# Five loads of 14, 9, 5, 3 and 1 row blocks in place of six of 10, 8, 6, 4, 2 and 2 for the last weight of a decode kernel

## The chip, the core and the metric

The kernel runs on one core of one Trainium2 chip. The metric is the time of one execution on the device, in microseconds (us); lower is better. Before the change three runs gave 127.64, 127.74 and 127.87 us, so the median is 127.74 us. A profile of one execution stands beside them. Engines are named as the profile names them: PE (TensorE, matmuls; PEld is its weight load), DVE (VectorE), ACT (ScalarE), POOL (GpSimd) and SP (SyncE, which here only issues loads). "SPq" is SP's instruction queue.

## The reference, cut to what matters

One token `x` of 576 numbers goes through two branches, and both results are added to it. Branch A is attention over the last 4096 positions of a cache with 16 key/value heads and 32 query heads; branch B is a gated feed-forward block. Everything is bf16 in memory.

```python
def _A_ref(x, k_cache, v_cache, wq, wo):
    q = (x @ wq) ...                                  # 32 heads of 128
    k = jnp.repeat(k_cache[:, :, Sk - W:, :], 2, axis=1)   # W = 4096
    v = jnp.repeat(v_cache[:, :, Sk - W:, :], 2, axis=1)
    p = _softmax(einsum('bhqd,bhkd->bhqk', q, k) * Dh ** -0.5)
    o = einsum('bhqk,bhkd->bhqd', p, v)
    return o.reshape(B, Sq, Hq * Dh) @ wo             # (1, 4096) @ (4096, 576)

def _B_ref(x, w_in, w_sp, b_sp, w_out):
    z = _gelu(x @ w_in)
    z1, z2 = z[..., :Fh], _layernorm(z[..., Fh:])     # Fh = 2304
    return (z1 * (w_sp * z2 + b_sp)) @ w_out          # (1, 2304) @ (2304, 576)

xn = _layernorm(x)
return x + _A_ref(xn, ...) + _B_ref(xn, ...)
```

The change concerns how `wo`, 4096 x 576, comes into the core. That matrix is the last thing the answer is multiplied with.

## The kernel before

**What is moved.** The core reads 50.96 MB: `wq`, `w_in`, 8 tiles of keys and 8 of values of 2048 KB each, `w_out` (2592 KB) and `wo` (4608 KB). One DMA moves one tile, every one of these is issued by SP, and all of them go through one queue (q1 in the profile). SP issues them in the order in which lines 98 to 111 write them: `wq`, two key tiles, `w_in`, keys and values in turn, `wout`, and last the pieces of `wo`.

**The ring.** All these tiles share a ring of 7 slots of 18 x 576 numbers per partition (`RING`, `SLOT`, the pool `ring`). A load past the seventh waits until an earlier tile's readers are done, and takes the slot that comes free. SP issues in order, so a load that waits holds back the loads behind it. In the profiled execution `wout` was issued at 81.44 us, when both value tiles of the second group of heads had been used, and the six pieces of `wo` at 85.86, 95.64, 100.32, 100.75, 113.93 and 114.35 us. They took the slots of key tile 6, key tile 7, value tiles 4 and 5, and value tiles 6 and 7, in that order: the first two waited for the transposes at line 268, the next two for the matmuls `pv(2)` at line 344, the last two for `pv(3)`.

**Row blocks of `wo`.** `load_n` (lines 93 to 96) views `wo` as 128 partitions x 32 row blocks x 576 columns. Partition p holds rows 32p to 32p+31; a row block t is row 32p+t of every partition. One row block is 128 x 1152 bytes, 144 KB. A load of n row blocks from `lo` on moves, for each partition, one run of n x 1152 bytes, starting lo x 1152 bytes into that partition's part of the matrix.

**What uses them.** The last stage of the kernel adds up the answer in two accumulators in PSUM, `acc[0]` for columns 0 to 287 and `acc[1]` for the rest. `out_mms` (lines 465 to 468) issues one matmul into each, at different columns of the PE array. For branch B `out_hv` does this for the 18 row blocks of `wout`; then lines 488 and 489 run over the 32 row blocks of `wo` in order, with `Y` (the attention result, its last quarter written by `y_copy(3)`) as the other operand. The first matmul of each piece waits for that piece's DMA. After the last one DVE and ACT copy the two halves of the answer to `res` (lines 492 and 493), SP stores it (line 494), and at line 520 SP waits once more for the counters of all queues and engines before the cores' engines meet at the end.

**Counters.** Each DMA signals a counter (semaphore). The loads of SP use eight counters in rotation; a DMA that uses all 16 DMA engines shows sixteen completions in the trace, one for each engine, and has landed with the last of them. The store of the answer, with one partition, ends with one completion.

Of the kernel before, what the change touches and what calls it, by code (L numbers as in the profile page):

```python
# [39 lines left out]
def kernel(  # L40
# [52 lines left out]
    def load_n(src, per, lo, n, name):  # L93
        v = ring_tile(f"{name}{lo}", n, D)
        nc.sync.dma_start(v, src.rearrange("(p t) n -> p t n", t=per)[:, lo:lo + n, :])
        return [(lo + t, v[:, t, :]) for t in range(n)]
# [10 lines left out]
        V[m] = load_kv(A_v_cache, m, "v")  # L107
    wout_sb = load_n(B_w_out, NF, 0, NF, "wout")
    wo_sb = []
    for n in (10, 8, 6, 4, 2, 2):  # L110
        wo_sb += load_n(A_wo, 32, len(wo_sb), n, "wo")


# [411 lines left out]
```

## Time and profile before

The profiled execution took 127.7 us on the device by its own clock; its span, from the first to the last instruction, is 125.9 us, and some 1.8 us lie around it. The median of the runs is 127.74 us.

| view | what it gives | value |
|---|---|---|
| busy time of the span | PE, DVE, ACT, POOL | 54%, 61%, 27%, 7% |
| DMA queues | q1's packets, as a share of 16 engines' span | 95.3% |
| stretches, 112 to 114 and 118 to 120 us | data moved | 422 and 415 GB/s |
| trace, last completion of `wout` | | 112.03 us |
| trace, last completion of the `wo` pieces of 10, 8, 6, 4, 2, 2 | | 115.28, 118.02, 120.08, 121.46, 122.14, 122.83 us |
| trace, median completion (8th of 16) of the same pieces | | 113.79, 116.50, 118.58, 120.03, 120.74, 121.41 us |
| timeline | first matmul with `wo`, last matmul ends | 116.89, 123.28 us |

How to read it: a row of forty digits has one digit for each fortieth of the span (3.15 us). The chain of waits follows the work that ended last back from the end, from each piece to what released it. A line of the timeline gives start, length, engine, line, operation and tiles, and in brackets how long the engine had been idle and what ended that.

### The profile page before, as it was taken

The numbers are of one execution on the slowest core, as the hardware profiler recorded it, in microseconds if no ns is written. First come the engines' busy times: TensorE is split into PE (matmuls) and PEld (weight loads), VectorE is DVE, ScalarE is ACT, GpSimd is POOL, SyncE is SP. The second block draws the span as 40 slices with busy tenths as digits, with TensorE's granted clock in tenths as the row PEclk, the third lists the DMA queues.
The fourth block names the chain that finished last, engine by engine and source line by source line (L and its number), as shares of the span: only waits on it lengthen the run. The fifth ranks groups of instructions, "written<-read, shape, count | busy, mean of one in ns | idle before, by whom it ended". The sixth has DMA issues, their size and how long they took to land.

```text
span 125.9 us, 1614 instructions
## 1 busy us (share of the span) xinstructions
PE 67.8 (54%) x618; PEld 30.9 (25%) x618; DVE 77.3 (61%) x149; ACT 33.6 (27%) x85; POOL 8.2 (7%) x28
## 2 busy tenths in 40 slices
PE   0002841089999977069356049648039711187861
PEld 0001301021299922014111012411012511024530
DVE  6704135999353896793898298899098967005001
ACT  1200011000036590000441930260950183910001
POOL 3991000000000000100000000000000000000000
PEclk9999999999996557856999959967756995559999
DMA  4999999999999999999999999999999999999950
GB/s 130 417 427 437 432 422 442 419 426 433 435 429 427 442 416 416 437 437 432 437 422 432 437 427 432 432 416 437 437 424 437 427 426 453 409 416 415 419 226 0
DMA packets 4127, 51.06 MB, mean 406 GB/s; under 512 B 534, under 2 KB 536, under 8 KB 1048
## 3 DMA queue, kind: packets, MB, share of 16 engines
q1 hardware_dynamic: 4034, 50.96, 95.3%
q8 instruction: 5, 0.08, 0.2%
q10 hardware_dynamic: 86, 0.00, 0.0%
q14 instruction: 2, 0.02, 0.0%
HBM read 50.96 MB, written 0.00 MB: 405 GB/s over the span
## 4 chain that ended last, share of the span: by engine, by line
DMA 56%; PE 16%; DVE 14%; ACT 7%; issue 3%; SPq 1%; POOL 0%; ACTq 0%
DMA k<-in_A_k_cache_dram 43%; DMA x<-in_A_x_dram 7%; DMA wo<-in_A_wo_dram 7%; DVE kT L268 6%; PE ops L344 6%; PE S L277 5%; ACT PT L321 4%; PE qps L227 3%; ACT pz L305 2%; DVE Qb L255 2%; DVE pt L315 2%; DVE q_rep L238 1%; ACT q_rep L236 1%; DVE on L358 1%; PE lps L327 1%
## 5 line engine op out<-in xcount | busy, mean ns | idle before, releaser
L277 PE MATMUL S<-kT,Qb 128*8 128x512 bf16 x128 | 32.5, 638 | 29.0 <-DVE kT L268 29.0
L268 DVE STREAM_TRANSPOSE kT<-k 128x1024 f32<-128x1024 f32 x32 | 36.9, 1212 | 6.9 <-DMA k<-in_A_k_cache_dram 6.8
L305 ACT ACTIVATE pz<-S,nm 64x1024 bf16<-64x1024 f32 x8 | 11.3, 1409 | 45.1 <-DVE nm L301 30.4
L321 ACT COPY PT<-pt 32x64 f32<-32x64 f32 x64 | 18.9, 296 | 14.3 <-DVE pt L315 13.6
L277 PEld LDWEIGHTS <-Qb 128*8 128x8 bf16 x128 | 6.4, 96 | 48.4 <-issue 45.4
L344 PE MATMUL ops<-v,PT 128*16 128x512 bf16 x128 | 11.7, 451 | 3.5 <-ACT PT L321 3.5
L315 DVE STREAM_TRANSPOSE pt<-pz 128x1024 bf16<-128x1024 bf16 x8 | 9.4, 1214 | 4.2 <-ACT pz L305 4.2
L380 PEld LDWEIGHTS <-win 128*128 128x128 bf16 x162 | 10.1, 169 | 0.9 <-issue 0.9
L380 PE MATMUL zps<-XT,win 128*128 128x2 bf16 x162 | 10.2, 202 | 0.0
L354 DVE SCALAR_TENSOR_TENSOR om<-ops,rs,dmask 128x512 f32<-128x512 f32 x4 | 3.0, 742 | 7.1 <-PE ops L344 7.1
L298 DVE TENSOR_REDUCE mx<-S 128x1 f32<-128x1024 f32 x4 | 4.9, 1222 | 3.8 <-PE S L277 3.8
L344 PEld LDWEIGHTS <-PT 128*16 128x16 bf16 x128 | 5.0, 98 | 7.4 <-ACT PT L321 4.1
L467 PE MATMUL acc<-wo,Y 128*1 128x288 bf16 x64 | 4.7, 285 | 1.7 <-DMA wo<-in_A_wo_dram 1.6
L194 PE MATMUL ps_x<-x,rmat 64*128 64x9 bf16 x1 | 0.2, 164 | 9.4 <-DMA x<-in_A_x_dram 9.4
L236 ACT CAST q_rep<-qps 128x512 bf16<-128x512 f32 x2 | 1.2, 585 | 14.7 <-DVE q_rep L238 14.7
L227 PE MATMUL qps<-wq,XT 128*2 128x512 bf16 x36 | 4.0, 626 | 1.0 <-DVE XT L218 1.0
L492 DVE CAST res<-acc 1x288 bf16<-1x288 f32 x1 | 0.4, 446 | 6.6 <-PE acc L467 6.6
L358 DVE TENSOR_REDUCE on<-om 128x128 f32<-128x512 f32 x4 | 4.1, 1036 | 0.1
L238 DVE CAST q_rep<-qps 128x512 bf16<-128x512 f32 x2 | 1.4, 692 | 4.6 <-PE qps L227 3.9
L327 PE MATMUL lps<-lx,lsum 128*128 128x1 f32 x8 | 2.2, 343 | 3.2 <-DVE Y L372 3.2
L493 ACT CAST res<-acc 1x288 bf16<-1x288 f32 x1 | 0.4, 389 | 12.7 <-PE acc L467 12.7
L467 PEld LDWEIGHTS <-Y 128*1 128x1 bf16 x64 | 2.8, 83 | 3.4 <-issue 2.5
(90 smaller groups left out, 44.6 us busy)
## 6 DMA issues: line engine op xcount, KB each, us to landing
k<-in_A_k_cache_dram SPq DMA_DIRECT2D x8, 2048.0 KB, 24.3
v<-in_A_v_cache_dram SPq DMA_DIRECT2D x8, 2048.0 KB, 24.8
win<-in_B_w_in_dram SPq DMA_DIRECT2D x3, 1728.0 KB, 23.3
wout<-in_B_w_out_dram SPq DMA_DIRECT2D x1, 2592.0 KB, 30.6
wq<-in_A_wq_dram SPq DMA_DIRECT2D x1, 2560.0 KB, 8.7
wq<-in_A_wq_dram SPq DMA_DIRECT2D x1, 2048.0 KB, 13.0
wo<-in_A_wo_dram SPq DMA_DIRECT2D x1, 1440.0 KB
wo<-in_A_wo_dram SPq DMA_DIRECT2D x1, 1152.0 KB
```

What stands on the lines that cost most here:

```text
L227: nc.tensor.matmul(qps[32 * g:32 * g + 2, :], lhsT=XT[:, s, :], rhs=wv[:, 512 * g:512 * (g + 1)], start=(s == 0), stop=(s == NS - 1), tile ...
L268: nc.vector.transpose(dst[:, 1024 * n:1024 * (n + 1)], src[:, 1024 * n:1024 * (n + 1)])
L277: nc.tensor.matmul(S[g % 2][32 * i:32 * i + 8, hf, :], lhsT=Qb[:, 2 * m + hd, be].rearrange("p a h -> p (a h)"), rhs=kv[:, be // 2, be % 2 ...
L298: nc.vector.tensor_reduce(out=mx[:, 0:1], in_=s[:], op=ALU.max, axis=mybir.AxisListType.XY)
L305: nc.scalar.activation(p[lo:hi, :, :, hd], s[lo:hi].rearrange("p a (t r) -> p (a t) r", r=16), ACT.Exp, bias=nm[lo:hi, 0:1], scale=SCALE, ...
L315: nc.vector.transpose(dst[:, 1024 * n:1024 * (n + 1)], src[:, 1024 * n:1024 * (n + 1)])
L321: nc.scalar.copy(PT4[32 * a:32 * a + 32, i % 2, i // 2, :], pt4[32 * i:32 * i + 32, :, a])
L327: nc.tensor.matmul(lps[:, 0:1], lhsT=lsum[:].rearrange("p q c x h -> p (q c x h)"), rhs=lx[:, g:g + 1], start=True, stop=True)
L344: nc.tensor.matmul(ops[32 * q:32 * q + 16, :], lhsT=d["PT"][:, pr, t0:t0 + 4].rearrange("p t x h -> p (t x h)"), rhs=V[2 * g + pr][:, t0:t ...
L358: nc.vector.reduce_sum(on[:], om[:].rearrange("p c d -> p d c"), axis=AXX)
L380: nc.tensor.matmul(zps[:, :, t], lhsT=wt[:, t, :], rhs=XT[:, s, :], start=(s == 0 and t == 0), stop=(s == NS - 1 and t == NF - 1), skip_gr ...
L467: nc.tensor.matmul(acc[n], lhsT=lhs[:, col:col + 1], rhs=wv[:, CW * n:CW * (n + 1)], start=False, stop=last, tile_position=(0, 32 * n))
```

## The change

One tuple of sizes at line 110 is replaced. The 32 row blocks are loaded in the same order and by the same queue, and the matmuls that use them stay in the same order.

```diff
     wo_sb = []
-    for n in (10, 8, 6, 4, 2, 2):
+    for n in (14, 9, 5, 3, 1):
         wo_sb += load_n(A_wo, 32, len(wo_sb), n, "wo")
```

The pieces begin at row blocks 0, 14, 23, 28 and 31, where they began at 0, 10, 18, 24, 28 and 30.

## The prediction

> **What bounds the kernel now.** I read the page's row of DMA shares first, then the chain of waits at its end, then the timeline of PE in the last 7 us, and last the closing waits of SP.
>
> ```profile
> DMA  4999999999999999999999999999999999999950
> q1 hardware_dynamic: 4034, 50.96, 95.3%
> q8 instruction: 5, 0.08, 0.2%
> ```
>
> The 16 DMA engines are full from the first slice to the 38th. What is loaded, not when it is asked for, sets the end. The chain ends so:
>
> ```profile
> 110.74 3.36 PE ops L344 x23
> ...
> 114.34 8.49 DMA wo<-in_A_wo_dram
> 122.83 0.04 issue
> 122.87 0.45 PE acc L467 x4
> 123.33 0.43 DVE res L492
> ```
>
> The chain walks from the last piece of wo back to its issue at 114.34 and from there to the matmuls of line 344, as if an earlier issue would help. It would not: 8.49 us is far more than 288 KB need. The piece stood in a full queue. The trace's completions show how that queue drains: wout's last completion at 112.03, then the six pieces' at 115.28, 118.02, 120.08, 121.46, 122.14, 122.83. The last five steps are 2.74, 2.06, 1.38, 0.68 and 0.69 us for 8, 6, 4, 2 and 2 row blocks: 0.343 us per row block each time, and no visible price of a piece. The earlier loads of 2048 KB end 4.85 us apart, 0.341 us for 144 KB. So the last byte arrives when the slowest DMA engine has worked off its share of everything.
>
> Now PE behind the landings:
>
> ```profile
> 116.89 2.37 PE L467 MATMUL acc<-wo,Y 128*1 128x288 bf16 x36
> 120.12 0.90 PE L467 MATMUL acc<-wo,Y 128*1 128x288 bf16 x12 [0.87 <-DMA wo<-in_A_wo_dram]
> 121.50 1.10 PE L467 MATMUL acc<-wo,Y 128*1 128x288 bf16 x12 [0.48 <-DMA wo<-in_A_wo_dram]
> 122.87 0.41 PE L467 MATMUL acc<-wo,Y 128*1 128x288 bf16 x4 [0.28 <-DMA wo<-in_A_wo_dram]
> ```
>
> PE needs 0.122 us for a row block (36 matmuls, 18 pairs, 2.37 us less the 0.29 of the last one, over 17 steps), a third of the 0.343 that the row block takes to arrive. It waits at each piece, starts 0.04 to 0.05 us after the landing, and finishes before the next. Only what it does after the last landing lies on the path.
>
> And the end, line 520:
>
> ```profile
> L520 SPq EVENT_SEMAPHORE  x7: 17/28/657, 124.2 to 125.8; - x7
> L520 SPq DRAIN  x3: 7/7/13, 125.2 to 125.5; - x3
> SPq L520 <- DMA out_dram<-res: 0.7, 1, 0.7
> ```
>
> The first five of these instructions check ten counters, two each, in a fixed order. The third (124.336, 0.657 long) contains the counter of the answer's store and waits for it until 124.993. The fourth and fifth, at 125.03 and 125.09, find all done, and the drain follows at 125.156.
>
> **The change part by part.**
>
> *Issue.* The pieces should take the slots in the order in which they came free before: 14 blocks at 85.86, 9 at 95.64, 5 at 100.32, 3 at 100.75, 1 at 113.93. Only one row block now waits for pv(3), instead of four. Worth nothing: at 113.93 the queue holds row blocks that keep it busy for 8 us more, and the fastest engine finished the piece of 4 blocks only at 119.51. The cover is that backlog; if it were gone, the piece issued at 113.93 would be late by its whole wait. One issue of SP (0.33 to 0.38 us) and its wait go away at 114.3, where SP has nothing to do until 123.79: zero. No wait is added, on SP, ACT's or POOL's queue.
>
> *The bytes* are the same, in the same order. One piece fewer saves eight packets' overhead and a completion on each engine. The slowest engine's steps give 0 for a piece; the mean over the sixteen completions gives 3.43, 2.75, 2.06, 1.40, 0.73 and 0.70 us, against 0.341 per row block 0.02 more for each large piece. I take -0.02 us; bounds 0 and -0.08 (a packet of 2304 bytes lasts 0.093 us in the trace but they follow each other every 0.086; eight such differences and a completion of 0.009 if none were hidden).
>
> *Small last packets.* The last piece's packets have 1152 bytes, and no load before has such. The nearest rows are the answer's store, one packet of 1152 bytes, 0.051 us, and the 2304-byte packets, 0.093 us: the difference is the bytes' time. So in proportion, 0; bounds 0 and +0.34 us, if 128 packets of 1152 bytes took as long as 128 of 2304 (0.685 a piece). I take 0, since the row of the right size lies on the line.
> In this trace every load starts at a multiple of 256 bytes (row blocks 0, 10, 18, 24, 28, 30; one is 4.5 x 256). The Trainium skill, "DMA: Bandwidth & Descriptors", section "How a descriptor splits into AXI transactions", speaks against the new cuts: a read that does not begin on a 256-byte boundary also fetches the bytes before it, and pays their beats. Row blocks 23 and 31 begin 128 bytes past one, so by the rule two pieces carry 128 bytes more in each packet, 8 x 128 bytes per engine, by the 2304-byte packets' pace some 0.038 us each, estimated: the sum would be 0.08 smaller, 127.58 us. No run here shows a load so placed.
>
> *Landings.* From 115.28 for ten blocks, at 0.343 a block: 14 blocks at 116.65, the second piece at 119.74, the third 121.46, the fourth 122.49, the last 122.83, less 0.02. PE is ready for wo at 116.89, so the larger first piece still comes 0.2 before it is wanted, and were it later PE has a second to catch up (14 x 0.122 from 116.89 ends at 118.6, the next landing is 119.74).
>
> *PE's tail.* Before: the last piece starts at 122.874, its second pair at 122.995, and the last matmul ends at 123.283. After: the piece of three starts 0.045 after 122.49, at 122.535, takes three pairs of 0.122 and frees PE at 122.90; the last row block has landed by then (122.83 + 0.045 = 122.875), so the last pair starts at 122.90 instead of 122.995. That is -0.095 us; bounds -0.12 (a pair) and 0. DVE, ACT and the store follow unchanged.
>
> *The closing waits.* The loads use eight counters in turn. With one DMA fewer, the store of the answer takes the counter that the last wo piece had before, one place earlier in the turn: not the one in the third check but one that sits in the fifth. If the order of checks stays, the first four are done during the store, and the drain comes 0.037 after the answer has landed (the gap behind an instruction here), at 124.993 + 0.037 = 125.03 instead of 125.156: -0.126 us. Bounds -0.126 and 0.
>
> Sum: -0.02 - 0.095 - 0.126 = -0.24 us. The profiled execution, 125.91 of span and 1.8 around it, 127.70 in all, would be 127.46; the median of the runs lies 0.04 above it, so 127.50, 0.19% faster. What a measurement of this kernel can tell from no change is about 0.2%, 0.26 us, so 127.48 divides "faster" from "same", and the forecast lies on that edge.
>
> **Rivals.** *The checks at the end follow the new order of counters.* For it: the order is chosen when the kernel is built, and the trace shows one instance. Then only -0.115 is left: 127.63 us.
>
> *Small packets cost a fixed time.* The last landing moves by +0.34 to 123.15, PE starts its last pair at 123.20 instead of 122.995, +0.2, less 0.126: 127.82 us, or 127.95 with the rival above as well. Against it: the 0.051 us packet. The Trainium skill's "Perfetto Trace Analysis", section "DMA Optimizations", says that DMAs under 2 KB pay a significant overhead per transfer; the packets' durations here do not bear that out.
>
> *A block of PE's code meets a late engine (slower).* Engines are not equally late. The sixteen completions of a load lay 0.52 us apart until 28 us and 1.45 us from 33 us on; the jump follows a packet of code at 29.63, and each 16 KB packet on q8 (36.33, 44.72, 77.98, 110.01) makes one more engine late. When wo ends, eleven engines are done by 121.65 and five at 122.28 to 122.83. The fifth such packet, at 121.55, delayed none, because its engine had finished. If the piece sizes put that block, or the moment PE asks for it, on one of the five while it still holds wo, a packet of that size on q1 lasts 0.61 us, so +0.6: 127.50 + 0.60 = 128.10 us. It decides from the point where the fetch comes before that engine's last wo packet. Against it: PE's instructions do not move, and with row blocks 23 to 27 released at 121.5 as 24 to 27 were, PE gets to the same place in the code at the same time or up to 0.12 later.
>
> *Nothing comes through* (the checks in new order and the last landing late by as much as PE gains) would be 127.74, and is inside the second and third.
>
> **How the numbers follow.** Chances: forecast 0.68, checks in new order 0.13, small packets 0.07, code 0.12. Around each lies the spread of the runs, 0.23 us over three. The forecast's own range is 127.35 to 127.62, and the low bounds of the packets and of PE's tail lie below the taken values, so I put 0.44 of its 0.68 under 127.48 and 0.24 over. The order of checks gives 0.02 and 0.11. Small packets: 0.05 same and 0.02 slower. Code: 0.12 slower. Together 0.46 faster, 0.40 same, 0.14 slower. The range leaves out the code case and the forecast's thin low end: 127.50 - 0.09 (the two unused bounds, 0.06 and 0.025) - 0.11 (half the spread) = 127.30; up to the small packets' 127.82, 127.85.
>
> **What would show it.** Five landings near 116.65, 119.74, 121.46, 122.49 and 122.81; PE idle before row blocks 14, 23 and 28, and not before 31; the last matmul ending near 123.17; the drain 0.04 after the landing of the answer. A last landing after 123.0 would make the prediction wrong: with equal steps in the sixteen completions it is packets, with one engine alone it is code. A gap in the DMA share before 121 us would say that the backlog argument is false.

## The result and the profile after

The changed kernel takes 127.50 us (median of 14 runs, 127.31 to 127.64) against 127.65 us for the kernel before (14 runs, 127.48 to 127.87) measured beside it: ratio 0.9984, interval 0.9977 to 0.9992. Two further comparisons gave 0.9985 (0.9973 to 0.9998) and 0.9983 (0.9973 to 0.9994). The medians differ by 0.15, 0.22 and 0.20 us, and three comparisons agree on a gain, though each alone is at the edge of what can be told.

The profiled execution took 127.54 us with a span of 125.66, against 127.70 and 125.91. First the page's rows of DMA share and of queues:

```profile
DMA  4999999999999999999999999999999999999960
q1 hardware_dynamic: 3890, 50.96, 95.5%
q8 instruction: 5, 0.08, 0.2%
```

The DMA engines are as full as before, up to the same slice. The packets on q1 fall from 4034 to 3890, by 144: one load fewer is 128 packets of data and 16 completions. Then the end of the chain of waits (start, length, what):

```profile
100.85 21.59 DMA wo<-in_A_wo_dram
122.44 0.04 issue
122.49 0.71 PE acc L467 x8
123.19 0.43 DVE res L492
```

The chain now goes back to the piece of three row blocks, issued at 100.85, not to the last one. The eight matmuls of the last two pieces follow each other without a gap that the chain shows: the last pair starts 0.133 us after the pair before it, where two pairs of one piece are 0.122 apart. The same in PE's timeline:

```profile
116.60 1.88 PE L467 MATMUL acc<-wo,Y 128*1 128x288 bf16 x28
119.67 1.27 PE L467 MATMUL acc<-wo,Y 128*1 128x288 bf16 x18 [1.18 <-DMA wo<-in_A_wo_dram]
121.41 0.78 PE L467 MATMUL acc<-wo,Y 128*1 128x288 bf16 x10 [0.47 <-DMA wo<-in_A_wo_dram]
122.49 0.66 PE L467 MATMUL acc<-wo,Y 128*1 128x288 bf16 x8 [0.30 <-DMA wo<-in_A_wo_dram]
```

PE waits before row blocks 14, 23 and 28, as forecast, and longer than before in sum (1.95 against 1.63 us); that idle time is not on the path. And the closing waits of SP at line 520 (count, then shortest, median and longest in ns):

```profile
L520 SPq EVENT_SEMAPHORE  x7: 17/28/28, 124.1 to 125.6; - x7
L520 SPq DRAIN  x3: 7/7/7, 124.9 to 125.2; - x3
```

with SP's wait for the answer's store in the view of waits (sum, number, longest):

```profile
SPq L520 <- DMA out_dram<-res: 0.6, 1, 0.6
```

None of the checks is 0.657 us long any more: the wait for the answer now lies before the fifth check, which is recorded with its own 28 ns, and the drain follows it.

The trace's own times, in us, side by side:

| | before | forecast | after |
|---|---|---|---|
| last completions of the pieces | 115.28, 118.02, 120.08, 121.46, 122.14, 122.83 | 116.65, 119.74, 121.46, 122.49, 122.81 | 116.54, 119.62, 121.36, 122.44, 122.82 |
| start of the last pair of matmuls | 122.995 | 122.90 | 122.863 |
| completion of the answer's store | 124.97 | | 124.83 |
| drain behind it | 125.156 | 0.04 after the store by the text, 0.06 by its figures | 124.914 |
| from the store's completion to the drain | 0.186 | | 0.081 |

### The profile page after: what moved, and what is told of

Its sections match the earlier page's. It is cut to its first block, busy times and chain, and to the rows that moved or that the text cites. A ratio compares the mean times of both kernels' runs of the same rounds, so it can differ in the third digit from the quotient of the medians.

```text
span 125.7 us, 1612 instructions
## 1 busy us (share of the span) xinstructions
PE 67.3 (54%) x618; PEld 30.8 (25%) x618; DVE 77.3 (62%) x149; ACT 33.6 (27%) x85; POOL 8.2 (7%) x28
## 3 DMA queue, kind: packets, MB, share of 16 engines
q1 hardware_dynamic: 3890, 50.96, 95.5%
## 4 chain that ended last, share of the span: by engine, by line
DMA 67%; PE 14%; DVE 12%; issue 3%; ACT 1%; SPq 1%; POOL 0%
DMA k<-in_A_k_cache_dram 43%; DMA wo<-in_A_wo_dram 17%; DMA x<-in_A_x_dram 7%; DVE kT L268 6%; PE S L277 5%; PE qps L227 3%; PE ops L344 3%; DVE Qb L255 2%; DVE q_rep L238 1%; ACT q_rep L236 1%; DVE on L358 1%; PE lps L327 1%; PE acc L467 1%; DVE om L354 1%; PE ps_x L204 0%
## 5 line engine op out<-in xcount | busy, mean ns | idle before, releaser
L344 PE MATMUL ops<-v,PT 128*16 128x512 bf16 x128 | 11.2, 430 | 3.5 <-ACT PT L321 3.5
```

The source lines that it names most:

```text
L344: nc.tensor.matmul(ops[32 * q:32 * q + 16, :], lhsT=d["PT"][:, pr, t0:t0 + 4].rearrange("p t x h -> p (t x h)"), rhs=V[2 * g + pr][:, t0:t ...
```

## The experiments

The differences are of the size of the spread, so each is read twice: in the times, and in the profile, where a step of 0.1 us is plain. Completions and starts that no view above prints are read from the same traces.

**Six loads with a one-block end, twice.** This has the new end and the old number of loads.

```diff
-    for n in (14, 9, 5, 3, 1):
+    for n in (13, 8, 5, 3, 2, 1):
```

> Six pieces of 13, 8, 5, 3, 2 and 1 row blocks: the number of loads of before, the one-block end of after. My theory (two gains, 0.1 us in PE's tail and 0.126 us in the closing waits): the last landing stays at 122.8, the last pair of matmuls starts 0.045 after it (122.87, against 122.995 before), but the store uses the third check's counter again and two checks follow its landing, so only the tail's gain is left: about -0.12 us against before, 127.53, ratio 0.9991. Rival (the closing waits give nothing, all of the gain is the shorter last piece): as fast as the changed kernel, -0.15 to -0.2 us, and the closing waits of the two look alike. Rival (the gain comes from having one load fewer, be it in the queue or at the end): no gain, 127.65, with a last landing as before or later.

> Pieces of 13, 8, 5, 3, 2, 1 once more: six loads, one-block end. Its first profile showed the tail's gain (last pair at 122.90 against 122.995) and its first times none. My theory (the gain in the tail is real and counts in the runs): ratio 0.999, 0.1 us behind the changed kernel. Rival (only the number of loads counts, the tail is lost in how the last landing scatters): ratio 1.0, as in its first runs, 0.15 us or more behind the changed kernel.

Measured: 127.69 us against 127.67, ratio 1.0000 (0.9991 to 1.0009), and the second time 127.55 against 127.76, ratio 0.9984 (0.9976 to 0.9993). The two do not agree with each other; my -0.12 us lies between them, and the times alone don't decide. Beside the changed kernel itself, measured with the second of them at 127.54, this one is 0.01 us behind, not the 0.1 that I expected. The profiles separate the two terms: last completions at 122.85 and 122.76, last pair 0.043 and 0.042 us later, as in the changed kernel (0.044; before 0.164). The closing check is the long one again, here the checks at line 520 in the first of the two profiles:

```profile
L520 SPq EVENT_SEMAPHORE  x7: 17/28/658, 124.1 to 125.7; - x7
```

From the store's completion to the drain it takes 0.186 and 0.185 us.

**Five loads with a two-block end, twice.** This has the old end and the new number.

```diff
-    for n in (14, 9, 5, 3, 1):
+    for n in (12, 8, 6, 4, 2):
```

> Five pieces of 12, 8, 6, 4 and 2 row blocks: the number of loads of after, the two-block end of before. My theory: the last pair of matmuls starts 0.12 us after the first pair of the last piece as before (122.99), the tail gains nothing; the store's counter sits in the fifth check, the drain comes 0.04 after that check ends, -0.126 us and some 0.02 for the piece: 127.51, ratio 0.9989. Rival (the one-block end is all of it): 127.65, ratio 1.0, with the drain 0.18 us after the answer's landing as before.

> Pieces of 12, 8, 6, 4, 2 once more: five loads, two-block end. Its first profile showed the closing checks in the order of the changed kernel, 0.126 us shorter. My theory: ratio 0.999, as the first time (0.9993). Rival (only the one-block end counts): ratio 1.0, as slow as before.

Measured: ratio 0.9993 (0.9984 to 1.0001), then 0.9988 (0.9979 to 0.9996), near the forecast 0.9989; beside the changed kernel's 127.54 the second is 127.61. In both profiles the last pair starts 0.16 us after the last completion (122.89 and 123.052; 123.16 and 123.32), as before the change, and the drain comes 0.08 us after the store, as after it. The checks at line 520 in the first of the two profiles:

```profile
L520 SPq EVENT_SEMAPHORE  x7: 17/28/28, 124.3 to 125.8; - x7
```

**The first piece in two loads.** Nothing in the program differs from the changed kernel but the number of loads, and through it the counter of the store.

```diff
-        nc.sync.dma_start(v, src.rearrange("(p t) n -> p t n", t=per)[:, lo:lo + n, :])
+        for a, b in ((0, 7), (7, 14)) if n == 14 else ((0, n),):
+            nc.sync.dma_start(v[:, a:b, :], src.rearrange("(p t) n -> p t n", t=per)[:, lo + a:lo + b, :])
```

The base, on the same chip:

> The changed kernel a third time, as the base of the next two. My theory: 0.15 to 0.25 us under before, ratio 0.998 to 0.9988.

> The changed kernel with its first piece of 14 row blocks loaded by two loads of 7 into the same tile, so that there are six loads again and nothing else differs at the end: same last landing, same tail. My theory: the store takes the third check's counter, two checks follow it, and the drain comes 0.126 us later after the answer's landing; the 7-block loads cost 0.02 us: 0.13 to 0.15 us behind the changed kernel, ratio to before about 0.9993. Rival (the checks' place is worth nothing in the times of whole runs): level with the changed kernel.

Measured: the base 127.54 us (0.9983), the split one 127.75 us (0.9999, interval 0.9989 to 1.0009): 0.21 us behind, where 0.13 to 0.15 were forecast. Its profile has the long check back (line 520 is 521 here):

```profile
L521 SPq EVENT_SEMAPHORE  x7: 17/28/655, 124.4 to 126.1; - x7
```

and 0.186 us from store to drain, which by the profiles is worth 0.186 - 0.081 = 0.105 us. I had expected the same end of the queue in both, and it was not the same: the last landing is at 123.16 in this profile and 123.05 in the base's, and the last pair starts 0.092 us after it instead of 0.041, because the last row block came only 0.315 us after the piece of three, less than PE needs for three pairs. So the whole runs are 0.21 us apart and agree with the closing checks, but they don't show that term alone; whether the split or the scatter of single executions moved the landing is open.

**One row block per load.** `load_n` issues one load for each number in `cuts`, all into one tile (its loop is left out of the cut below).

```diff
+        cuts = {14: (5, 5, 4), 5: (1,) * 5, 3: (1,) * 3}.get(n)
+        wo_sb += load_n(A_wo, 32, len(wo_sb), n, "wo", cuts)
```

> The changed kernel with the same five tiles, but the last nine row blocks come by nine loads of one row block each (packets of 1152 bytes, every second one starting 128 bytes past a 256-byte boundary), and the first tile by three loads, so that there are thirteen loads and the store keeps the counter it has after the change. My theory (a packet costs its bytes, a load some 0.01 to 0.02 us): steps of 0.343 to 0.36 us between the last completions of the nine, last landing 122.8 to 123.0, 127.5 to 127.7 us. Rival (reads that start off a 256-byte boundary pay for the bytes before it): the steps of row blocks 23, 25, 27, 29, 31 are about 0.038 us longer than those of 24, 26, 28, 30, +0.2 us in all. Rival (a small packet costs as much as one of 2304 bytes): steps near 0.68 us, the last landing 3 us later, 130.5 us.

Measured: 128.64 us, ratio 1.0072 (1.0058 to 1.0085), so the time missed my forecast. The steps up to row block 29 did not. From 119.78 the last completions lie at 120.15, 120.53, 120.88, 121.26, 121.64, 122.02 and 122.41: row blocks 23, 25, 27 and 29 took 0.37, 0.35, 0.38 and 0.39 us, row blocks 24, 26 and 28 took 0.38 each. A row block alone costs 0.376 us against 0.343 in a large piece, so a load of 1152-byte packets costs 0.03 us more than its bytes. It does not cost 0.685, and odd row blocks are not dearer than even ones. The Trainium skill's rule on reads that start off a 256-byte boundary ("DMA: Bandwidth & Descriptors", section "How a descriptor splits into AXI transactions"), which by estimate would have added 0.038 us to each odd one, does not show here; the trace decides against it at this size of packet. In the changed kernel's own trace all packets of 1152 bytes last 0.051 us, those of row block 31, which starts off such a boundary, too.

Then row blocks 30 and 31 come late. SP's waits (times in us: sum, number, longest) and PE's timeline:

```profile
SPq L97 <- DMA wo<-in_A_wo_dram: 6.4, 4, 2.8
SPq L97 <- DMA wout<-in_B_w_out_dram: 6.0, 1, 6.0
```

```profile
119.82 2.92 PE L472 MATMUL acc<-wo,Y 128*1 128x288 bf16 x32 [0.76 <-DMA wo<-in_A_wo_dram]
123.66 0.64 PE L472 MATMUL acc<-wo,Y 128*1 128x288 bf16 x4 [0.91 <-DMA wo<-in_A_wo_dram]
```

With thirteen loads on eight counters, SP holds each of the later loads until the load that had its counter has landed. Row block 30 was issued at 119.80, right after the nine-block piece had landed on its counter at 119.78. Its first completion came 0.85 us after that of row block 29, where 0.38 is the pace: the early engines had run dry. This is what becomes of the cover when the backlog is gone. Its last completion came 1.20 us after that of row block 29, but that is one engine of the sixteen, 0.84 us behind all others (123.61; the next at 122.77, which is on pace). So most of the time lost, 0.84 of some 1.1 us, is that one engine, and the nine small loads at 0.03 us each make up the rest, as an estimate; the engines that ran dry did not set the landing. A code packet started at 121.36; that it is what held the late engine fits the executions below, but the trace names no engine for a packet.

**More code for PE.** 60 matmuls with a zero column, which add zeros to the answer, in the step `j == 10` of the loop (the lines that set up the column `zz` are left out).

```diff
+        if j == 10:
+            for i in range(60):
+                nc.tensor.matmul(acc[i % 2][:, 0:128], lhsT=zz[:, 0:1], rhs=ident[:],
+                                 start=False, stop=False, tile_position=(0, 32 * (i % 2)))
```

> The changed kernel with 60 further matmuls of a zero column (120 PE instructions) in the tenth step of the loop, where PE has idle time; they add zeros to the answer. Their code moves every later 16 KB packet of code to an earlier time, the fifth one from 110 to 100 or before and the sixth from 121 to 110 or so. My theory (each such packet makes one DMA engine late by 0.5 to 0.7 us, and one not late before, as all so far did): six late engines at the end instead of five, the last landing within 0.1 us of 122.82, 127.4 to 127.7 us. Rival (such a packet can fall on an engine that is late already): five late engines, one of them 0.6 us later, last landing 123.4, 128.1 us. Rival (code packets have nothing to do with late engines): five late engines and the same end.

Measured: 127.57 us, 0.9992 (0.9983 to 1.0002), last landing 122.92. The fourth 16 KB packet came at 91.50 and the fifth at 119.62, where the changed kernel's first profile has them at 110.43 and 120.70 (the expectation counts the 8 KB packet at 29 us too, so they are its fifth and sixth; the last came later than its 110). At the end six engines are more than 1.2 us behind the first, where the changed kernel has five (counting one at 1.02). How far each of the sixteen is behind the first, in us, the six latest, from this kernel's completions:

```text
load landed at  90.88:  0.52 0.62 1.37 1.64 1.68 1.69
load landed at  95.78:  0.74 1.29 1.52 1.57 1.58 1.63   (a code packet at 91.50, another of 8 KB at 93.74)
load landed at 119.48:  0.55 1.31 1.47 1.57 1.59 1.61
load landed at 121.65:  1.28 1.47 1.55 1.58 1.61 2.03   (a code packet at 119.62)
load landed at 122.92:  1.29 1.48 1.59 1.61 1.62 1.87
```

After each of these two 16 KB packets one more engine is late, as the theory said, and the first of these steps moved from 110 to 91.5 with its packet. But what it costs that engine is some 1.5 us (by the rows, an estimate: one near 0.5 has gone, one at 2.03 has come), not the 0.5 to 0.7 of my expectation, and the last one fell behind all others, so a late packet set the landing (122.92; the others were done at 122.67).

**The changed kernel once more**, on the chip of the two repeats above.

> The changed kernel once more, beside the next two on the same chip, since the differences are of the size of the spread. My theory: -0.15 to -0.25 us against before (ratio 0.998 to 0.999), and 0.1 us ahead of each of the next two. Rival (the change is worth nothing and the first comparison was chance): ratio 0.9995 to 1.0005.

Measured: 127.54 us, 0.9985 (0.9973 to 0.9998). Its profiled execution was its slowest, 128.10 us, with a last landing at 123.45 instead of 122.82:

```profile
120.33 1.27 PE L467 MATMUL acc<-wo,Y 128*1 128x288 bf16 x18 [1.23 <-DMA wo<-in_A_wo_dram]
122.12 0.78 PE L467 MATMUL acc<-wo,Y 128*1 128x288 bf16 x10 [0.52 <-DMA wo<-in_A_wo_dram]
123.14 0.65 PE L467 MATMUL acc<-wo,Y 128*1 128x288 bf16 x8 [0.24 <-DMA wo<-in_A_wo_dram]
```

Every landing is 0.6 to 0.7 us later than in the first profile of the same kernel, and the completions, given as above, say from where:

```text
load landed at 105.69:  0.60 0.76 0.94 1.28 1.60 1.61 1.91
load landed at 112.41:  0.59 0.74 1.26 1.63 1.64 1.89 2.48   (a code packet at 109.80)
load landed at 123.45:  0.59 0.72 1.26 1.64 1.65 1.89 2.48
```

The engine at 0.94 is gone and one at 2.48 has come: the packet met an engine that was already behind, so it need not make one more engine late. In the first profile the packet of that time met one of the early engines, and the last engine stayed at 1.78. Which engine it meets differs between executions of one kernel.

**An uneven load.** The three-block piece by partitions 0 to 87 and 88 to 127.

```diff
-        nc.sync.dma_start(v, src.rearrange("(p t) n -> p t n", t=per)[:, lo:lo + n, :])
+        rows = src.rearrange("(p t) n -> p t n", t=per)
+        for p0, p1 in ((0, 88), (88, P)) if lo == 28 else ((0, P),):
+            nc.sync.dma_start(v[p0:p1], rows[p0:p1, lo:lo + n, :])
```

> The changed kernel with the piece of three row blocks loaded by two loads, partitions 0 to 87 and 88 to 127. By the Trainium skill (DMA: Bandwidth & Descriptors, section on why a DMA increments its semaphore by 16) a load of 88 partitions uses the 11 lowest engines and one of 40 the 10 lowest, so engines 11 to 15 would carry nothing of this piece and engines 0 to 9 half as much again, 0.5 us. The look is to show whether the five late engines are among the low ones. If all five are: eleven completions for the first part with five late ones, the last landing 0.5 us later, 128.0 us. If none is: no late one among the eleven, the late engines skip 1.03 us, last landing about 122.3, 127.0 us. Rival (all 16 engines take part in any load): sixteen completions each, nothing moves.

One run: 129.43 us, slower than either forecast. The two parts had eleven and ten completions of data, as the Trainium skill's page says ("DMA: Bandwidth & Descriptors", the section on why a DMA increments its semaphore by 16). But the completions did not keep their order of lateness: already the five-block piece ahead, which was not touched, ended at 122.88 instead of 121.36, with 3.32 us between its first and last engine. So the run doesn't tell whether the late engines are among the low ones, and why the load ahead spread out so much stays open.

**The store issued by ACT.**

```diff
-    nc.sync.dma_start(out.flatten_outer_dims(), res[:])
+    nc.scalar.dma_start(out.flatten_outer_dims(), res[:])
```

> The changed kernel with the store of the answer issued by ACT, which makes one half of it, instead of SP. My theory: ACT's copy ends 0.02 us before DVE's, the issue still waits for DVE, and SP's counter check before it falls away, so the store starts up to 0.05 us earlier; it ends on a counter of ACT's loads, whose place among the checks decides: 0.1 us faster than the changed kernel if it is the last, 0.1 slower if two checks follow. Rival (the issue on ACT takes as long as on SP and the place is the same): level.

Measured: 127.48 us, 0.9981 (0.9970 to 0.9993), beside 127.54 and 0.9983 for the changed kernel: not to be told apart, as the rival said. The store did not start earlier (0.076 us after DVE's copy ends, 0.074 in the changed kernel's first profile), and it sits on the same last counter as when SP issues it, so ACT's issues take their counters from the same rotation; the drain comes 0.08 us after it in both. The kernel beats the one before, and is no proven gain over the change.

## Why the prediction was right, point by point

The forecast was 127.50 us and -0.24 us; the runs gave 127.50 and, over the three comparisons, -0.15, -0.22 and -0.20 us. In the profiled span the change is -0.25 us. That the median is met to the hundredth is luck: the kernel before measured 0.09 us less than the 127.74 from which the forecast started, and the gain beside it was 0.09 less than forecast. The span is met by luck in part: the last landing of the changed kernel is at 122.82, 123.45 and 123.05 in its three profiles, and the first of them happens to match the 122.83 before. By the prediction's own sign, a last landing after 123.0, the other two would have spoken against it; the sign took no account of this scatter. What is not luck is the two steps behind the last landing, which the experiments show one by one.

- **The bound.** The queue is full and drains at one rate, so the last landing does not depend on the pieces. Right for the mean of the sixteen completions of the last piece: 121.69 before; 121.68, 121.79 and 121.78 after; 121.77 and 121.69 with six other pieces, 121.68 and 121.69 with five. The last completion scatters more than any cut moved it: 122.83 before; 122.82, 123.45 and 123.05 after; 122.85 and 122.76 with six pieces, 122.89 and 123.16 with five. In the first profile the forecast of the five landings is off by 0.01 to 0.12 us.
- **Issue and backlog.** Worth nothing while the backlog covers it. Right; the one-row loads show the other case, where a load issued 2.6 us ahead of the end of the backlog left the early engines without work for some 0.5 us (0.85 less 0.38).
- **One piece fewer, small packets.** -0.02 and 0 were taken; -0.01 is the difference of the two landings in the first pair of profiles, far inside their scatter. A piece of one row block costs 0.03 us more than its bytes, which takes back the piece saved. The bound of -0.08 does not follow from its working: eight times 0.007 and 0.009 are 0.065.
- **PE's tail.** -0.095 was taken, with -0.12 as a bound; the start of the last pair against its last landing went from 0.164 to 0.044, which is -0.120. The small last piece is the cause: the step is there with six pieces and a one-block end (0.043, 0.042) and gone with five and a two-block end (0.165, 0.164). The forecast had PE busy until 122.90; the piece of three landed at 122.44, not 122.49, so PE was free in time and only the last landing counted. That is close: with a last row block 0.315 us behind the piece of three, in the kernel with the split first piece, 0.092 was left.
- **The closing waits.** -0.126 was taken, -0.105 is measured. The order of the checks stayed, and the store's counter moved from the third to the fifth. In all thirteen profiles the drain comes 0.185 or 0.186 us after the store's completion where the counter is in the third check, and 0.081 or 0.082 where it is in the fifth. What I left out is the fifth check itself, which still has to run after the wait (0.028 us); and the 124.993 from which I counted is the end of the third check, 0.023 after the landing.
- **The three terms** are 0.01, 0.120 and 0.105 in the first pair of profiles, together 0.24 us; the whole runs gave a little less. The store's own duration differs by less than 0.01 us between the two profiles (from its issue to its completion 1.13 us in each).
- **The rival of the code packets** was mis-sized and partly misplaced. A 16 KB packet costs an engine some 1.5 us (0.94 to 2.48 above), not 0.6, and not only the one at 121 us can hurt: in the execution that landed at 123.45 the one at 110 decided how late the last engine was. PE did not ask for the fifth packet "at the same time or up to 0.12 later" than 121.55: it came at 120.70, 121.42 and 121.11 in three executions of the changed kernel, and it delayed no piece in them. Nothing here shows that the change has a part in it; the rival belongs, as far as these runs tell, to the scatter of single executions.
- **The rival of small packets** is ruled out at its price of 0.34 us (0.03 measured).

## What to carry to other kernels

Where a queue is full to the end, cutting its last loads differently moves only what comes after the last landing: make the last piece so small that little is left to do once it has landed, but not so small that it lands before the engine behind it is done with the piece ahead. Count the loads too: they are dealt to a fixed number of counters (eight here), and a store that falls on the counter which is checked last saves the checks behind it, while a load that needs a counter still in use waits for it. Before believing 0.1%, look for it in the trace as a step at one place; two comparisons of one kernel here gave 1.0000 and 0.9984.

## What the runs showed that I had not expected

In the executions read here, packets of PE's code hold up the DMA engines that carry the data: when more code for PE moved a 16 KB packet from 110 to 91.5 us, the step in the lateness moved with it. One such packet sets its engine back by some 1.5 us, of which little is made up before the end (0.3 us in the kernel before, 2.17 to 1.88 behind the first engine). In before and after alike eleven engines are done about 1.2 us before the last one, and the last one sets the time: in the changed kernel's first profile the mean completion of the last piece is 121.68, the last 122.82. That 1.1 us is far more than the 0.24 us of this cut, and how to share the load unevenly to win it is open.
